# Landing tiles of an attention-and-FFN kernel laid out at a pitch of 256 bytes a row

## The chip, the cores and the metric

One core of a Trainium2 chip runs the whole program. The metric is the device time of one execution in microseconds (us). Fast runs of one kernel beside each other differ by 0.3% to 1.5% here, so each ratio below has its 95% interval. On one core there is no second die to compare with, so a run counts as slow when it is more than 1.5% above the fastest of the same kernel.

## The reference

The first half is a gated linear recurrence over 768 tokens, for 4 batches of 8 heads of width 48. The second half is a feed-forward net with a squared ReLU over the 3,072 resulting rows of 384 numbers.

```python
f = 1 / (1 + exp(-f_logit))                       # all of shape [4, 8, 768, 48], float32
for t in range(768):
    state = f[:, :, t, :, None] * state + k[:, :, t] (outer) v[:, :, t]
    y[:, :, t] = q[:, :, t] @ state
x = y.transpose(0, 2, 1, 3).reshape(3072, 384)
out = (relu(x @ w_in) ** 2) @ w_out               # w_in [384, 2048], w_out [2048, 384]
```

## The kernel before

The kernel works on 24 chunks of 128 tokens. For each chunk it loads four tiles (f, k, q, v), each by one DMA issued from SyncE. A partition holds one token, and the token's 8 heads are 8 rows of 48 floats. In HBM these 8 rows lie far apart (the layout is batch, head, token, width), so **every load is 1,024 separate rows of 192 bytes**, 64 for each of the 16 DMA engines. In SBUF the 8 rows of a token follow one another without gaps, 1,536 bytes in all. There are six buffers for each of the four tiles.

```python
C, H, D, DP = 128, 8, 48, 64
const = ctx.enter_context(tc.tile_pool(name="const", bufs=1))
io = ctx.enter_context(tc.tile_pool(name="io", bufs=IOB))          # IOB = 6
wst = ctx.enter_context(tc.tile_pool(name="wst", bufs=WSTB))
...
def load(i):
    b, c = divmod(i, NC)
    for n in ("f", "k", "q", "v"):
        def fn(n=n):
            t = io.tile([C, H, D], F32, tag="io_" + n, name="io_" + n)
            nc.sync.dma_start(t, srcs[n][b].rearrange("h s d -> s h d")[c * C:(c + 1) * C])
            st[n, i] = t
...
# the readers of the four tiles
nc.scalar.activation(e, st["f", i].rearrange("p h d -> p (h d)"), AFT.Exp, scale=-1.0)
nc.gpsimd.tensor_copy(vz[i % 3], st["v", i])
nc.vector.tensor_mul(az[i % 2][:, H:, :D], st["k", i], st["ep", i])
nc.vector.tensor_mul(az[i % 2][:, :H, :D], st["q", i], st["en", i][:, :HD].rearrange(...))
```

A planner in the kernel orders all steps ahead of time, so that attention chunks, the two matmuls of the net (`hp`, line 429, and `op`, line 474) and the weight loads interleave. The order on each engine is fixed when the program is built.

The tile pools are laid out one behind the other, and nothing rounds them to more than 32 bytes. The constants end at byte 52,896 of a partition, which is 206 × 256 + 160. All 24 landing tiles therefore begin at 160 modulo 256.

## Time and profile before

| | |
|---|---|
| time, median of 3 runs | 201.05 us (200.92 to 201.1) |
| span of the profiled run | 200.3 us |
| TensorE (PE) busy | 92% of the span |
| loads of f, k, q, v | 96 × 192 KB = 18.9 MB of the 29.9 MB in the queue |
| last of these loads issued | at 128.0 us |

These lines are from the page of the kernel before. The first two are 40 equal slices of the span, 5 us each: the busy share of the DMA engines in tenths, and the GB/s they moved. Then come the DMA queue (packets, MB, share of the 16 engines' span), two groups of instructions (busy us, mean ns of one | idle time before them and what ended most of it) and two of the DMA issues (the last number is the median us from issue to landing).

```profile
DMA  6999989899979999999989999931101111101012
GB/s 127 188 163 306 370 152 197 210 373 246 196 155 230 188 223 173 220 164 195 196 176 202 212 194 196 183 72 44 39 3 39 39 43 41 39 14 40 37 70 79
...
q1 hardware_dynamic: 107008, 29.89, 71.9%
...
L283 POOL CAST vz<-io_v 128x384 bf16<-128x384 f32 x24 | 14.7, 613 | 69.3 <-DMA io_v<-in_v_dram 50.6
L278 ACT ACTIVATE e<-io_f 128x384 f32<-128x384 f32 x24 | 12.6, 525 | 18.4 <-DMA io_f<-in_f_logit_dram 18.2
...
io_f<-in_f_logit_dram SPq DMA_DIRECT2D x24, 192.0 KB, 4.7
...
io_v<-in_v_dram SPq DMA_DIRECT2D x24, 192.0 KB, 4.5
```

For 130 us the DMA engines are nearly always busy, and then they have next to nothing to do. While they move rows of 192 B they reach about 150 to 230 GB/s. While they move the weights, in pieces of 1.5 to 2 KB, they reach about 370. ScalarE waits 18.2 us in all for f. GpSimd waits much longer for v, but it has little else to do.

The table by stretches of the same kernel gives the start and end of a stretch in us, its length, the busy us of PE (with the number of instructions) and of the other engines, the granted clock, the DMA share and GB/s. The DMA share adds up the times of the packets, which overlap, so it can be over 1.

```profile
core 0: us, PE busy (x) PEld busy (x) DVE busy (x) ACT busy (x) POOL busy (x), PEclk, DMA share, GB/s
...
48.00:78.00 30.00, 29.06 (x364) 20.84 (x363) 26.19 (x53) 21.16 (x46) 8.77 (x16) 1.00 1.00 191
78.00:106.00 28.00, 26.74 (x302) 18.16 (x300) 25.08 (x53) 22.55 (x51) 7.87 (x15) 1.00 1.03 191
106.00:130.00 24.00, 22.98 (x229) 15.05 (x228) 20.06 (x43) 17.22 (x40) 4.57 (x8) 1.00 1.18 197
```

Both TensorE and the DMA engines are close to full from 48 to 130 us. TensorE is the main limit, but it waits some 3.2 of these 82 us. This line of the timeline of SyncE's queue (start, duration) is the last load:

```profile
128.00 0.77 SPq L205 DMA_DIRECT2D io_v<-in_v_dram  x1
```

### The profile page before, as it was taken

The numbers are of one execution on the slowest core, as the hardware profiler recorded it, in microseconds if no ns is written. First come the engines' busy times: TensorE is split into PE (matmuls) and PEld (weight loads), VectorE is DVE, ScalarE is ACT, GpSimd is POOL, SyncE is SP. The second block draws the span as 40 slices with busy tenths as digits, with TensorE's granted clock in tenths as the row PEclk, the third lists the DMA queues.
The fourth block names the chain that finished last, engine by engine and source line by source line (L and its number), as shares of the span: only waits on it lengthen the run. The fifth ranks groups of instructions, "written<-read, shape, count | busy, mean of one in ns | idle before, by whom it ended". The sixth has DMA issues, their size and how long they took to land.

```text
span 200.3 us, 5054 instructions
## 1 busy us (share of the span) xinstructions
PE 183.7 (92%) x1965; PEld 128.5 (64%) x1965; DVE 141.1 (70%) x302; ACT 131.8 (66%) x279; POOL 39.5 (20%) x80
## 2 busy tenths in 40 slices
PE   5976898769989998999998999999999999999993
PEld 5855787657856665666665666666765666666651
DVE  3577878869869999898987779998855854333300
ACT  4462786669866578987977668678766565665410
POOL 5143001610133433114143031231400200000000
PEclk9999999999999999999999999999999999999999
DMA  6999989899979999999989999931101111101012
GB/s 127 188 163 306 370 152 197 210 373 246 196 155 230 188 223 173 220 164 195 196 176 202 212 194 196 183 72 44 39 3 39 39 43 41 39 14 40 37 70 79
DMA packets 107031, 30.20 MB, mean 151 GB/s; under 512 B 100352, under 2 KB 105472, under 8 KB 107008
## 3 DMA queue, kind: packets, MB, share of 16 engines
q1 hardware_dynamic: 107008, 29.89, 71.9%
q8 instruction: 15, 0.25, 0.5%
q14 instruction: 8, 0.07, 0.1%
HBM read 25.17 MB, written 4.72 MB: 149 GB/s over the span
## 4 chain that ended last, share of the span: by engine, by line
PE 45%; DMA 27%; SPq 19%; ACT 3%; issue 2%; POOL 1%; DVE 1%; POOLq 0%; ACTq 0%
PE op L474 20%; SPq L205 18%; PE hp L429 17%; DMA io_v<-in_v_dram 16%; DMA io_f<-in_f_logit_dram 11%; PE tr L321 2%; PE yp L359 2%; PE at L336 1%; SPq L221 1%; POOL vz L283 1%; PE pc L289 1%; ACT e L278 1%; PE xp L373 1%; ACT pz L279 1%; PE ds L390 1%
## 5 line engine op out<-in xcount | busy, mean ns | idle before, releaser
L429 PE MATMUL hp<-xT,w_in 128*128 128x384 bf16 (+2 forms) x528 | 78.9, 282 | 5.8 <-ACT hr L436 3.7
L474 PE MATMUL op<-w_out,hT 128*128 128x384 bf16 x384 | 77.5, 326 | 0.0
L436 ACT ACTIVATE hr<-hp 128x384 bf16<-128x384 f32 (+1 forms) x94 | 47.4, 509 | 22.7 <-PE hp L429 21.5
L429 PEld LDWEIGHTS <-w_in 128*128 128x128 bf16 x528 | 42.7, 98 | 23.2 <-issue 4.8
L445 DVE TENSOR_TENSOR hT<-hr 128x384 bf16<-128x384 bf16 (+1 forms) x91 | 34.9, 385 | 28.0 <-ACT hr L436 26.6
L474 PEld LDWEIGHTS <-hT 128*128 128x128 bf16 x384 | 35.4, 98 | 21.9 <-issue 1.0
L343 DVE TENSOR_TENSOR am<-at,ut 128x512 bf16<-128x512 f32 x48 | 31.7, 683 | 1.8 <-PE at L336 1.4
L407 POOL TENSOR_TENSOR sz<-tm,en 48x192 bf16<-48x192 f32 x40 | 21.5, 539 | 46.8 <-DVE tm L398 28.5
L283 POOL CAST vz<-io_v 128x384 bf16<-128x384 f32 x24 | 14.7, 613 | 69.3 <-DMA io_v<-in_v_dram 50.6
L278 ACT ACTIVATE e<-io_f 128x384 f32<-128x384 f32 x24 | 12.6, 525 | 18.4 <-DMA io_f<-in_f_logit_dram 18.2
L309 DVE TENSOR_TENSOR az<-io_k,ep 128x384 bf16<-128x384 f32 x24 | 13.7, 573 | 5.7 <-ACT ep L299 4.2
L321 PE MATMUL tr<-ident,az 128*128 128x128 bf16 x192 | 15.8, 223 | 1.4 <-DVE az L313 1.3
L438 DVE TENSOR_SCALAR hr<-hp 128x384 bf16<-128x384 f32 (+1 forms) x26 | 15.2, 588 | 2.2 <-PE hp L429 2.1
L443 ACT ACTIVATE hT<-hr 128x384 bf16<-128x384 bf16 (+1 forms) x29 | 15.9, 548 | 0.9 <-DVE hr L438 0.3
L321 PEld LDWEIGHTS <-az 128*128 128x128 bf16 x192 | 12.3, 100 | 4.4 <-DVE az L313 2.1
L327 DVE COPY ts<-tr 128x1024 bf16<-128x1024 bf16 x20 | 13.7, 684 | 1.7 <-PE tr L321 1.6
L313 DVE TENSOR_TENSOR az<-io_q,en 128x384 bf16<-128x384 f32 x24 | 14.1, 588 | 1.0 <-ACT en L305 0.7
L484 ACT COPY ob<-op 128x384 f32<-128x384 f32 x18 | 8.6, 477 | 9.4 <-PE op L474 9.3
L299 ACT ACTIVATE ep<-pc 128x384 f32<-128x384 f32 x24 | 11.7, 488 | 3.6 <-PE pc L292 3.6
L503 PE MATMUL idle<-zero 128*128 128x128 bf16 x141 | 13.1, 246 | 1.0 <-DVE zero L248 1.0
L279 ACT ACTIVATE pz<-e 128x384 bf16<-128x384 f32 x24 | 12.5, 523 | 0.8
L305 ACT ACTIVATE en<-pc 128x388 f32<-128x388 f32 (+1 forms) x24 | 11.9, 495 | 0.0
(43 smaller groups left out, 157.9 us busy)
## 6 DMA issues: line engine op xcount, KB each, us to landing
io_f<-in_f_logit_dram SPq DMA_DIRECT2D x24, 192.0 KB, 4.7
io_k<-in_k_dram SPq DMA_DIRECT2D x24, 192.0 KB, 4.5
io_q<-in_q_dram SPq DMA_DIRECT2D x24, 192.0 KB, 4.6
io_v<-in_v_dram SPq DMA_DIRECT2D x24, 192.0 KB, 4.5
out_dram<-ob SPq DMA_DIRECT2D x24, 192.0 KB, 1.9
wi_f<-in_moe_w_in_dram SPq DMA_DIRECT2D x4, 768.0 KB, 7.8
wo_f<-in_moe_w_out_dram SPq DMA_DIRECT2D x4, 768.0 KB, 8.1
```

What stands on the lines that cost most here:

```text
L205: nc.sync.dma_start(t, srcs[n][b].rearrange("h s d -> s h d")[c * C:(c + 1) * C])
L278: nc.scalar.activation(e, st["f", i].rearrange("p h d -> p (h d)"), AFT.Exp, scale=-1.0)
L283: nc.gpsimd.tensor_copy(vz[i % 3], st["v", i])
L321: nc.tensor.transpose(tr[:, y, :], a[:, 2 * y:2 * y + 2, :].rearrange("p h d -> p (h d)"), ident)
L343: nc.vector.tensor_mul(t, st["at", i][x], ut4)
L407: nc.gpsimd.tensor_mul(nx[r, :, D * x:D * (x + 1)], st["tm", i][r, :, D * x:D * (x + 1)], st["en", i][r, HD:HD + NP].unsqueeze(2).to_broad ...
L429: nc.tensor.matmul(hp[:, x, :], w_in[:, ks, (f + x) * C:(f + x + 1) * C], xT[:, ks, lo:lo + W], start=(ks == 0), stop=(ks == KS - 1), skip ...
L436: nc.scalar.activation(hr[:, :m, :], st["hp", c0, f][:, :m, :], AFT.Relu)
L438: nc.vector.tensor_scalar_max(hr[:, :m, :], st["hp", c0, f][:, :m, :], 0.0)
L443: nc.scalar.activation(st["hT", g][:, f:f + m, lo:lo + W], hr[:, :m, :], AFT.Square)
L445: nc.vector.tensor_mul(st["hT", g][:, f:f + m, lo:lo + W], hr[:, :m, :], hr[:, :m, :])
L474: nc.tensor.matmul(st["o", i], hT[:, fs, tt * C:(tt + 1) * C], w_out[:, fs, :], start=(fs == 0), stop=(fs == FS - 1))
```

## The change

The intent is that every row of 192 bytes begins at a multiple of 256 bytes in SBUF, so that no row is cut by a 256-byte line. The landing tile gets 64 floats a head instead of 48, and the last 16 stay unused. The activation of f can no longer read its tile as one flat run, so it takes 8 runs of 48.

```diff
-                t = io.tile([C, H, D], F32, tag="io_" + n, name="io_" + n)
+                t = io.tile([C, H, DP], F32, tag="io_" + n, name="io_" + n)[:, :, :D]
                 nc.sync.dma_start(t, srcs[n][b].rearrange("h s d -> s h d")[c * C:(c + 1) * C])
...
-            nc.scalar.activation(e, st["f", i].rearrange("p h d -> p (h d)"), AFT.Exp, scale=-1.0)
+            nc.scalar.activation(e.rearrange("p (h d) -> p h d", d=D), st["f", i], AFT.Exp, scale=-1.0)
```

## The prediction

> **What bounds the kernel now.** The change touches the 96 loads of q, k, v and f (18.9 of 29.9 MB) and their readers. In the timeline of the SyncE queue the last load is issued at 128.0 us. Until then the slices of the page show the DMA engines mostly at 90% or more, and the chain of waits gives 27% of the span to DMA and 18% to issuing loads. After 130 us only TensorE matters. But it is nearly full before too: in the table by stretches it is busy 29.1 of 30 us at 48-78 us, 26.7 of 28 at 78-106, 23.0 of 24 at 106-130. Counting matmul columns at the tail's rate (163 ns for 384), it does 92-93% of its possible work in those 82 us; gaps over 0.15 us sum to 4.4 us. So much faster loads would win some 4 us there, and an estimated 2 to 6 us in the first 48 us.
>
> **What the change does.** Number, size and order of the packets, their HBM addresses and the instruction order stay; only SBUF addresses move. The Trainium skill ("DMA: Bandwidth & Descriptors", How a descriptor splits into AXI transactions) says that transactions are cut at 256 B and that a read not starting at a multiple of 256 B fetches from the boundary below: the hope behind the change. Two things speak against it:
>
> 1. The tiles don't begin at a multiple of 256. In the address map of the program before, all 24 landing tiles begin at 160 modulo 256, and tiles of 2,048 B are not aligned either (az at 43,936). Rows now begin at 160, 96, 32 and 224: three of four cross a 256-byte line. With the padding I expect all at 160 and all to cross. The alignment would not be reached; any cost of crossing would grow.
>
> 2. Crossing shows no cost. Of 98,304 packets of 192 B in the trace's records 68,656 (70%) took the same 15 ns, which could not be if three of four paid a second transaction. At 50-60 us, with the queue not backed up, 0 to 4% are over 17 ns; where many loads are queued (8-12, 120-124 us) 70% are: slowness follows load, not address. At the start one engine begins a packet every 11.8 ns, through all four offsets.
>
> **Readers.** The activation of f becomes 8 runs of 48: ScalarE's other one of the pair already writes such runs, in 523 ns against 525 (the costliest groups). VectorE's products (573, 588 ns) and GpSimd's cast (613 mean, 512 median) read 8 runs instead of one: an estimate of 0 to 20 ns each, under 1 us of VectorE in all, off the chain. GpSimd is 20% busy.
>
> **Predicted time.** 201.2 us, 8 in 10 between 200.3 and 202.4. Faster by over 2%: 0.03; within 2%: 0.93; slower by over 2%: 0.04.
>
> **What would show it.** Packets of 192 B keep their peak at 15 ns and their mean of 18 (+-0.7) ns; issue to landing stays 4.4-4.8 us; last load issued at 127-130 us; TensorE's busy time in the three stretches within 0.5 us; the activation of f within 10 ns of 525, the cast within 30 ns of its mean.
>
> **What would make it wrong.** Writes that drain behind the records: if the slow 30% come from SBUF writes cut in two, crossing all rows would add some 5% to the loads (an estimate: a quarter more crossings at 3.5 ns, over 18 ns), 2 to 4 us. Had the allocator aligned the tiles after all, the same mechanism would win as much. An issue of the padded pattern that takes SyncE much longer than now (0.65 to 1.1 us) would also delay loads.

## The result, and the profile after

| | before | after |
|---|---|---|
| time, median of 4 runs | 200.99 us | 207.48 us (207.38 to 208.79) |
| ratio of the fast runs | 1 | 1.0344 (1.0299 to 1.039) |
| span of the profiled run | 200.3 us | 205.6 us |
| packets of 192 B: mean | 18.0 ns | 22.3 ns |
| packets of 192 B that took 15 ns | 70% | 44% |
| last load issued | 128.0 us | 134.6 us |

A ratio here is the mean time of one kernel's fast runs over that of the other's of the same rounds, so it is not quite the ratio of the medians beside it. The packet figures are counted from the trace's records of single DMA packets.

The kernel got 3.4% slower. All its engines run the same instructions in the same order as before, so only durations and waits can differ. These are the same lines of the page after.

```profile
DMA  7999999999989999999999999991011110101122
GB/s 120 163 142 273 380 166 176 157 386 269 196 164 201 195 199 168 191 175 198 164 191 175 203 175 175 193 169 44 0 41 38 38 38 5 40 36 41 38 77 77
...
q1 hardware_dynamic: 107008, 29.89, 83.4%
...
L283 POOL CAST vz<-io_v 128x384 bf16<-128x384 f32 x24 | 15.0, 626 | 78.9 <-DMA io_v<-in_v_dram 46.6
...
L278 ACT ACTIVATE e<-io_f 128x384 f32<-128x384 f32 x24 | 12.6, 525 | 24.1 <-DMA io_f<-in_f_logit_dram 24.0
...
io_f<-in_f_logit_dram SPq DMA_DIRECT2D x24, 192.0 KB, 5.1
...
io_v<-in_v_dram SPq DMA_DIRECT2D x24, 192.0 KB, 5.0
```

The number of packets and the bytes are the same, and the time that the packets took rose from 71.9 to 83.4% of a longer span. The readers did not change: the activation of f takes 525 ns as before, and the cast of v 626 against 613. ScalarE now waits 24.0 us for f instead of 18.2. A load takes 5.0 to 5.2 us to land instead of 4.5 to 4.7.

The table by stretches after:

```profile
core 0: us, PE busy (x) PEld busy (x) DVE busy (x) ACT busy (x) POOL busy (x), PEclk, DMA share, GB/s
...
48.00:78.00 30.00, 27.59 (x354) 19.90 (x352) 24.42 (x50) 19.82 (x43) 7.84 (x13) 1.00 1.16 193
78.00:106.00 28.00, 26.07 (x282) 17.39 (x281) 24.79 (x52) 21.72 (x50) 7.11 (x14) 1.00 1.38 180
106.00:130.00 24.00, 22.12 (x224) 14.40 (x222) 18.41 (x40) 17.60 (x41) 4.96 (x9) 1.00 1.23 182
```

And the last load, in the timeline of SyncE's queue:

```profile
134.59 1.16 SPq L205 DMA_DIRECT2D io_v<-in_v_dram  x1
```

TensorE lost 1.5, 0.7 and 0.9 us of work in these three stretches. Together with the three stretches before 48 us it was busy 116.7 us of the first 130 before and 111.3 after, which is 5.4 us less. From 130 to 150 us TensorE is busy without a gap in both kernels (20.00 of 20 us), and the missing work is simply done later: the span grew by 5.3 us. (The medians are 6.5 us apart. The profiled execution of the kernel before took 202.05 us, 1 us over its median.) So the time went into slower loads, and it reached the end through work that TensorE could not yet do.

### The profile page after: what moved, and what is told of

Its sections match the earlier page's. It is cut to its first block, busy times and chain, and to the rows that moved or that the text cites. A ratio compares the mean times of both kernels' runs of the same rounds, so it can differ in the third digit from the quotient of the medians.

```text
span 205.6 us, 5054 instructions
## 1 busy us (share of the span) xinstructions
PE 183.6 (89%) x1965; PEld 127.2 (62%) x1965; DVE 141.8 (69%) x302; ACT 131.5 (64%) x279; POOL 39.4 (19%) x80
## 3 DMA queue, kind: packets, MB, share of 16 engines
q1 hardware_dynamic: 107008, 29.89, 83.4%
## 4 chain that ended last, share of the span: by engine, by line
PE 46%; DMA 25%; SPq 21%; ACT 3%; issue 2%; POOL 1%; DVE 1%; POOLq 0%; ACTq 0%
PE op L474 21%; SPq L205 20%; PE hp L429 17%; DMA io_v<-in_v_dram 12%; DMA io_f<-in_f_logit_dram 8%; DMA wo_f<-in_moe_w_out_dram 5%; PE tr L321 2%; PE at L336 1%; PE yp L359 1%; SPq L221 1%; POOL vz L283 1%; PE xp L373 1%; PE pc L289 1%; ACT e L278 1%; PE ds L390 1%
## 5 line engine op out<-in xcount | busy, mean ns | idle before, releaser
L429 PEld LDWEIGHTS <-w_in 128*128 128x128 bf16 x528 | 42.7, 98 | 22.3 <-issue 3.5
L321 PEld LDWEIGHTS <-az 128*128 128x128 bf16 x192 | 11.9, 98 | 4.6 <-DVE az L313 1.9
L289 PE MATMUL pc<-pz,ut 128*128 128x384 bf16 x24 | 7.9, 328 | 7.7 <-ACT pz L279 4.5
L503 PE MATMUL idle<-zero 128*128 128x128 bf16 x141 | 12.2, 235 | 1.0 <-DVE zero L248 1.0
```

What stands on the lines that cost most here:

```text
L321: nc.tensor.transpose(tr[:, y, :], a[:, 2 * y:2 * y + 2, :].rearrange("p h d -> p (h d)"), ident)
L429: nc.tensor.matmul(hp[:, x, :], w_in[:, ks, (f + x) * C:(f + x + 1) * C], xT[:, ks, lo:lo + W], start=(ks == 0), stop=(ks == KS - 1), skip ...
```

## The experiments

A row of 192 bytes that begins at byte r of a 256-byte line crosses into the next one when r is over 64. With tiles at 160 modulo 256, the rows of the kernel before begin at 160, 96, 32 and 224 in turn, and **three of four cross**. At a pitch of 256 they all begin at 160, and **all cross**. The address map of the program after shows this: its 24 landing tiles still begin at 160 modulo 256. The change did not do what it set out to do.

Three theories of the slowdown were tested:

- **A.** A row that crosses a 256-byte line in SBUF costs the writing side of a DMA engine more.
- **B.** Boundaries of 64 bytes matter. All rows of both kernels begin off them.
- **C.** The gaps or the power-of-two pitch cost, wherever the rows begin.

The first four kernels ran beside the kernel before (median 201.03 us of 7 runs).

### Padded, tiles at 0 modulo 256

The edit to the changed kernel puts 96 unused bytes ahead of the landing tiles, and 160 behind so that everything else keeps its place modulo 256.

```diff
+    sh1 = ctx.enter_context(tc.tile_pool(name="sh1", bufs=1))
+    sh1.tile([C, 24], F32, name="sh1")
     io = ctx.enter_context(tc.tile_pool(name="io", bufs=IOB))
+    sh2 = ctx.enter_context(tc.tile_pool(name="sh2", bufs=1))
+    sh2.tile([C, 40], F32, name="sh2")
```

> The change with its landing tiles begun at 0 modulo 256 instead of 160 (96 unused bytes ahead, 160 behind so that nothing else moves): rows at 0, none crosses a 256-byte line. Theory A (a row that crosses a 256-byte line costs the DMA engine extra): mean packet of 192 B down to 15-16 ns, time 197 to 200 us, faster than before, since no row crosses instead of three of four. Theory B (a row not on a 64-byte boundary costs): the same as A here. Theory C (landing with gaps, at a pitch of 256 B, costs, wherever the rows begin): still 206 to 208 us and a mean packet of 22 ns.

Measured: 197.49 us, ratio to before 0.9783 (0.9705 to 0.9861), with one of its four runs (201.17 us) slow and left out of the ratio. The mean packet took 15.5 ns. From its page:

```profile
GB/s 130 215 171 356 337 182 196 291 378 146 211 164 194 231 213 172 232 205 212 198 197 235 198 218 213 123 12 34 40 40 16 27 42 43 40 40 40 30 54 80
...
q1 hardware_dynamic: 107008, 29.89, 65.0%
...
L282 ACT ACTIVATE e<-io_f 128x384 f32<-128x384 f32 x24 | 12.6, 526 | 8.8 <-DMA io_f<-in_f_logit_dram 8.8
...
io_v<-in_v_dram SPq DMA_DIRECT2D x24, 192.0 KB, 3.8
```

With 96 bytes of filler the same padded kernel goes from 3.4% slower to 2.2% faster than before. The wait for f falls to 8.8 us, and a load lands in 3.8 us. Theory C is refuted: pitch and gaps are the same as in the slow version. So is another fear of the prediction, that SyncE takes longer to issue the padded pattern: its issues of v took 0.81 us (median) before, 1.03 after the change, and 0.80 here with the same pattern.

### Padded, tiles at 128 modulo 256

The edit is the same with 224 bytes ahead and 32 behind. Every row crosses, and every row begins on a 64-byte boundary.

> The change with its landing tiles begun at 128 modulo 256: every row crosses a 256-byte line, and every row begins on a 64-byte boundary. Theory A (256-byte lines): as slow as the change, 206 to 208 us, mean packet 21 to 23 ns. Theory B (64-byte boundaries): as fast as with tiles at 0, 197 to 200 us. Theory C (pitch): 206 to 208 us.

Measured: 207.82 us, ratio 1.0321 (1.0266 to 1.0375), mean packet 21.8 ns.

```profile
q1 hardware_dynamic: 107008, 29.89, 81.6%
...
io_v<-in_v_dram SPq DMA_DIRECT2D x24, 192.0 KB, 5.1
```

It is as slow as the change. Theory B alone is refuted.

### A pitch of 320 bytes

The edit to the changed kernel is one number. The tiles begin at 160 as in the change, and the rows begin at 160, 224, 32 and 96: the four offsets of the kernel before, but with gaps.

```diff
-                t = io.tile([C, H, DP], F32, tag="io_" + n, name="io_" + n)[:, :, :D]
+                t = io.tile([C, H, 80], F32, tag="io_" + n, name="io_" + n)[:, :, :D]
```

> The change with rows at a pitch of 320 B instead of 256, tiles at 160 modulo 256: rows begin at 160, 224, 32 and 96, the four offsets of the kernel before, but with gaps between the rows as in the change. Theory A: three of four cross, as before: 200 to 202 us, mean packet 18 ns. Theory B: as before too. Theory C (gaps): 206 to 208 us.

Measured: 200.89 us, ratio 1.0002 (0.993 to 1.0074), mean packet 18.6 ns. Gaps, larger tiles and readers with 8 runs show no cost together. The share of crossing rows is enough to give the old time.

### Unpadded, tiles at 0 modulo 256

The edit is that of the first experiment (96 bytes ahead, 160 behind), made to the kernel before. Two of four rows cross.

> The kernel before, unpadded, with its landing tiles begun at 0 modulo 256: rows at 0, 192, 128 and 64, so two of four cross a 256-byte line instead of three, and all begin on 64-byte boundaries. Theory A: mean packet near 16.5 ns, between that with tiles at 0 padded and that of before, 198 to 200.5 us. Theory B: as fast as the padded kernel with tiles at 0. Theory C: as before, 201 us.

Measured: 196.8 us, ratio 0.9787 (0.9726 to 0.9847), mean packet 15.5 ns.

```profile
q1 hardware_dynamic: 107008, 29.89, 65.7%
...
L282 ACT ACTIVATE e<-io_f 128x384 f32<-128x384 f32 x24 | 12.6, 526 | 9.7 <-DMA io_f<-in_f_logit_dram 9.7
...
io_v<-in_v_dram SPq DMA_DIRECT2D x24, 192.0 KB, 3.7
```

This was not foreseen by A in its simple form: with half the rows crossing, the loads were as fast as with none. B would explain it, but B alone had just failed. Either both boundaries matter, or the cost of crossing is hidden as long as few enough rows cross. The loads alone and the padded tiles at 32 tell these apart.

### Loads alone

This is a kernel without arithmetic, whose output is zeros and so wrong. Sixteen stages of 24 loads follow one another, of the same form as in the kernel, and the stages differ only in where the rows begin.

```python
for name, src, off, pitch in STAGES:
    for j in range(24):
        a = ...     # the load's 128 x 8 rows of 192 B in HBM
        t = slots[j][:, off // 4:off // 4 + 8 * pitch // 4].rearrange("p (h w) -> p h w", w=pitch // 4)[:, :, :48]
        nc.sync.dma_start(t, a)
```

> No arithmetic and a wrong result on purpose: 16 stages of 24 loads each, back to back, each load 128 partitions of 8 rows of 192 B as in the kernel; the stages differ only in where a row begins in SBUF (0, 32, ... 224 modulo 256 at a pitch of 256; a pitch of 192 from 0 and from 160) and in HBM (back to back as now; at a pitch of 256 from 0, 64, 128). Theory A (a row that crosses a 256-byte line in SBUF costs the writing side of an engine more; hidden while the mean stays below what the reading side needs): a load takes some 0.9 to 1.0 us with rows at 0, 32 and 64, 10 to 25% more with rows at 96 to 224 (all cross), 0 to 3% more at pitch 192 from 0 (two of four cross), 3 to 8% more at pitch 192 from 160 (three of four). Theory B (64-byte boundaries as well): rows at 32 slower than at 0 and 64 by 5% or more, and rows at 128 and 192 faster than at 96, 160 and 224. If the reading side is the floor and pays for crossings in HBM, rows that cross none there are faster than now by 5% or more with rows at 0 in SBUF, and rows that all cross there are slower.

From its table by stretches, one row inside each stage (DVE and POOL do nothing; the last two numbers are the DMA share and GB/s). The first nine rows are: pitch 256 from 0, 32, 64, 96, 128, 160 and 224 modulo 256, then pitch 192 from 0 and pitch 192 from 160. The next two have rows at 0 in SBUF while in HBM they are at a pitch of 256 from 0 (no row crosses there) and from 128 (all cross there). The last row repeats the first stage.

```profile
core 0: us, DVE busy (x) POOL busy (x), PEclk, DMA share, GB/s
6.00:22.00 16.00, 0.00 (x0) 0.00 (x0) 1.00 1.09 215
28.00:44.00 16.00, 0.00 (x0) 0.00 (x0) 1.00 1.07 210
50.00:66.00 16.00, 0.00 (x0) 0.00 (x0) 1.00 1.09 214
77.00:95.00 18.00, 0.00 (x0) 0.00 (x0) 1.00 1.54 163
105.00:124.00 19.00, 0.00 (x0) 0.00 (x0) 1.00 1.53 163
134.00:152.00 18.00, 0.00 (x0) 0.00 (x0) 1.00 1.51 163
...
192.00:210.00 18.00, 0.00 (x0) 0.00 (x0) 1.00 1.50 163
217.00:233.00 16.00, 0.00 (x0) 0.00 (x0) 1.00 1.10 211
240.00:258.00 18.00, 0.00 (x0) 0.00 (x0) 1.00 1.39 187
...
264.00:280.00 16.00, 0.00 (x0) 0.00 (x0) 1.00 1.05 213
...
338.00:352.00 14.00, 0.00 (x0) 0.00 (x0) 1.00 1.14 217
...
388.00:404.00 16.00, 0.00 (x0) 0.00 (x0) 1.00 1.09 214
```

A load is 196,608 bytes, so 215 GB/s is 0.915 us a load, 163 is 1.205 us and 187 is 1.05 us. The step lies between rows at 64 and rows at 96, where 192 bytes begin to cross a line. On either side of it the starting byte makes no difference that shows: 32 is within 2.5% of 0 and 64, and 128 is as bad as 96, 160 and 224. That settles A against B. (Rows that cross nothing all take the 0.915 us of a floor that the last run of loads explains, so a smaller effect of the first byte could be hidden there.) The sizes given to A were too small: all rows crossing cost 32% where 10 to 25% were expected, three of four 15% where 3 to 8% were. What the rows do in HBM shows no effect at this rate.

The numbers also suggest why half the rows may cross for nothing. All rows crossing take 1.205 us / 64 = 18.8 ns a row and engine. If a row that crosses nothing takes half, 9.4 ns, then three of four give 16.5 ns, or 1.054 us a load, and 1.05 was measured. Two of four give 14.1 ns, or 0.904 us, which is just under the 0.915 us that a load takes anyway.

### Padded, tiles at 32 modulo 256

The edit is the same with 128 bytes ahead and 128 behind. No row crosses, and none begins on a 64-byte boundary.

> The change with its landing tiles begun at 32 modulo 256: no row crosses a 256-byte line, none begins on a 64-byte boundary. Theory A: as with tiles at 0, 196 to 198.5 us, mean packet 15.5 ns. Theory B, or a mix in which 64-byte boundaries matter too (which would explain why unpadded tiles at 0 did as well as padded ones): 199 us or more, mean packet over 16.5 ns.

Measured beside the kernel before (201.29 us): 197.09 us, ratio 0.9774 (0.9723 to 0.9824), mean packet 15.5 ns. In the whole kernel too, 64-byte boundaries don't matter.

### Unpadded, tiles at 0, and the weights' tiles too

The edit to the kernel before is its shortest good form: the two lines of `sh1` alone.

> The unpadded kernel with landing tiles at 0 modulo 256, the filler of 160 bytes behind them left out, so that the weights' staging tiles begin at 0 modulo 256 too. It repeats the best version in its simplest form. Theory A: 196 to 198 us; the eight weight loads gain at most a nanosecond or two of 84 a packet, so no more than 0.5 us better than with the filler.

Measured: 197.71 us, ratio 0.9795 (0.9743 to 0.9847). Moving the weights' staging tiles to 0 modulo 256 adds nothing that can be seen.

### Shares of crossing rows

Loads alone again (wrong output), with 0, 3, 4, 5, 6, 7 and 8 of 8 rows crossing, by pitches of 256, 272, 192, 288, 192, 272 and 256 from suitable bytes. After these come stages with loads issued by SyncE and ScalarE in turn.

> Loads alone again, a wrong result on purpose: 12 stages of 24 loads, with 0, 3, 4, 5, 6, 7 and 8 of a load's 8 rows a partition crossing a 256-byte line (by pitch and first byte), and four of these shares again with the loads issued by SyncE and ScalarE in turn. From the first measurement alone (0.915 us a load with no row crossing, 1.205 with all) the model is: the writing side takes 9.4 ns for a row that crosses no line and twice that, 18.8, for one that does, and a load takes the larger of 64 rows of that mean and a floor of 0.915 us. It expects, in us a load: 0.92 with 0, 3 and 4 of 8 crossing, 0.98 with 5, 1.05 with 6, 1.13 with 7, 1.205 with 8. Rival: the cost is not additive but a matter of some threshold or pattern; then 5, 6 and 7 of 8 lie off that line by over 0.02. For the floor: if it is SyncE's issuing, two queues bring none crossing down to 0.75-0.85 us and 4 of 8 only to 0.90; if it is the engines' reading, two queues leave both at 0.91-0.93. 8 of 8 stays at 1.205 in either case.

From its table by stretches, the rows for 4, 5, 6 and 7 of 8:

```profile
51.00:67.00 16.00, 0.00 (x0) 0.00 (x0) 1.00 1.07 212
73.00:90.00 17.00, 0.00 (x0) 0.00 (x0) 1.00 1.10 201
97.00:114.00 17.00, 0.00 (x0) 0.00 (x0) 1.00 1.43 187
122.00:142.00 20.00, 0.00 (x0) 0.00 (x0) 1.00 1.48 174
```

| crossing, of 8 | model, us a load | measured, 196,608 B over the GB/s |
|---|---|---|
| 0 | 0.92 | 0.93 |
| 3 | 0.92 | 0.93 |
| 4 | 0.92 | 0.93 |
| 5 | 0.98 | 0.978 |
| 6 | 1.05 | 1.051 |
| 7 | 1.13 | 1.130 |

The sum holds: 9.4 ns for a row, 18.8 for a crossing one, and a floor below which crossings are hidden. The other stages of this run failed as a measurement. ScalarE had nothing to wait for and issued its share of the later stages early, so that they mixed with the stage of 8 of 8. Their numbers are not used.

### What the floor is

This is the same kind of kernel with every load issued by SyncE and ScalarE in turn from the first on, in four pairs of stages.

```diff
-            nc.sync.dma_start(t, a)
+            (nc.scalar if j % 2 else nc.sync).dma_start(t, a)
```

> Loads alone, every load issued by SyncE and ScalarE in turn from the first on (in the run before, ScalarE's loads ran ahead into the stage of another share and mixed them). Pairs of stages of 24 loads: no row crossing, 4 of 8, 8 of 8, none again. If the floor of 0.915 us a load is one queue's issuing: none crossing 0.60 to 0.85 us a load, and 4 of 8 at 0.90 (64 rows of 14.1 ns), so that crossings show at half the rows too. If the floor is the engines' own reading: 0.91 to 0.93 for both. 8 of 8 stays at 1.205.

From its table by stretches: none crossing, 4 of 8, 8 of 8, and none again.

```profile
4.00:19.00 15.00, 0.00 (x0) 0.00 (x0) 1.00 1.28 259
...
62.00:79.00 17.00, 0.00 (x0) 0.00 (x0) 1.00 1.40 218
85.00:108.00 23.00, 0.00 (x0) 0.00 (x0) 1.00 1.51 163
...
160.00:174.00 14.00, 0.00 (x0) 0.00 (x0) 1.00 1.28 259
```

With two queues, none crossing takes 0.76 us a load, 4 of 8 takes 0.90 and 8 of 8 takes 1.205 as ever. So the floor of 0.915 us belongs to the use of one queue. Whether it is SyncE's own time to issue or something else in the queue is not shown: a second engine and a second queue came in together. Once the floor is gone, crossings cost at half the rows too, by the amount that the sum gives (0.904). What limits the loads at 0.76 us (11.9 ns a row) stays open: it is above the 0.60 us that 9.4 ns a row would allow.

### Padded and unpadded at 0, five rounds

The last two runs are the kernels of the first and the fourth experiment again, on one chip, with the kernel before at 200.25 us.

> The padded kernel with tiles at 0 modulo 256 again, beside the unpadded one with tiles at 0, on one chip: by the model their loads take the same (none and two of four rows crossing both lie at or under the floor of 0.915 us), so 196 to 198.5 us and within 0.5% of each other.

> The unpadded kernel with tiles at 0 modulo 256 again: 196 to 198.5 us, within 0.5% of the padded one. If it is clearly slower, half the rows crossing costs something in the kernel after all; if clearly faster, the padding costs something else (readers of 8 runs).

Measured: padded 196.77 us, ratio 0.9833 (0.9779 to 0.9888); unpadded 196.06 us, ratio 0.9796 (0.9747 to 0.9846). The intervals overlap, so no difference is shown, and the padding has nothing to its credit. Two lines that move the tiles by 96 bytes give all of the gain, at no cost in SBUF worth naming. The unpadded kernel with tiles at 0 is the one to keep. It beats both the kernel before and the change. (Each of these kernels is clearly faster than the one before, but every interval includes 0.98, so a gain of over 2% is not shown.) With two issuing queues the padding might earn its place, since none crossing then took 0.76 us a load against 0.90 with half; that was not tried in the whole kernel.

## Why the prediction was wrong

**Point 1 was right.** The prediction said from the address map that the tiles begin at 160 modulo 256, that the change would not align them and that all rows would cross instead of three of four. They do.

**Point 2, "Crossing shows no cost", is the step that failed.** It read the packet records: 70% of the packets took 15 ns, which "could not be if three of four paid a second transaction". That inference is unsound. In the changed kernel every row crosses, and still 44% of the packets took 15 ns. So the record of a single packet does not show what its own row costs. That the cost appears on other packets, as delay once the writing side is behind, fits this but is inferred: no record here separates reading from writing. "Slowness follows load, not address" could not be concluded either. Every stretch of the kernel before has the same mix, three of four rows crossing, so comparing its stretches says nothing about addresses. The packet every 11.8 ns "at the start" may show only how fast packets begin before the queue is full: with two queues each engine took 11.9 ns a row that crosses nothing. The reading that shows the cost is the rate where the queue is full, set beside that of other addresses. The second slice (5 us) of the page shows 188 GB/s before, 163 after and 215 with padded tiles at 0; the loads alone ran at 187, 163 and 215 with three of four, all and none crossing. The prediction had only the first of these rates; a kernel with other addresses was needed to read it.

**The fallback had the mechanism and too small a size.** "What would make it wrong" named writes cut in two and estimated 3.5 ns a crossing, 5% on the loads and 2 to 4 us. The runs gave 9.4 ns more for a crossing row and 1.05 to 1.205 us a load, which is 15%; the kernel lost 6.5 us. A quarter more crossings at 9.4 ns is 2.4 ns over 16.4, or 14%.

**How much of it reached the end.** The fallback's 5% are some 5 us of DMA time (96 × 1.05 × 0.05), of which it let 2 to 4 us, 40% to 80%, reach the end. The runs are at or just under the low end of that. Loads that are 15% longer are 96 × 0.155 = 15 us more of DMA time, of which 6.5 us (43%) reached the end. Fixed alignment saves 96 × 0.13 = 12 us of DMA time, of which 4.2 us (35%) reached the end (2.1% of 201.03 us by the ratio). The prediction's gain for much faster loads, some 4 us in the stretch of 48 to 130 us plus 2 to 6 us before it, was not tested: these loads were only 12% faster.

**Readers: right.** The activation of f stayed at 525 ns, and the cast of v moved by 13 ns. The other tests that the prediction set (mean packet, landing, last load, TensorE's busy time in the stretches) all failed in the direction of slower loads; only the commonest packet stayed at 15 ns.

The Trainium skill ("DMA: Bandwidth & Descriptors", How a descriptor splits into AXI transactions) says that transactions are cut at 256 B. The prediction cited it and then argued it away. The runs agree with a cut at 256 bytes on the SBUF side: twice the time (18.8 against the fitted 9.4 ns) as soon as a row of 192 bytes crosses, whatever the sizes of the two pieces (163 GB/s from 96, 128, 160 and 224 alike). That the doubling is one transaction against two is what the page suggests; no run here shows transactions as such.

## What to carry to other kernels

For loads in short rows, look at the byte address modulo 256 at which each row lands, in the program's address map, and count the rows that cross: a pitch aligns nothing unless the first byte is aligned, and here, with rows of 192 bytes, the only length measured, 96 bytes of filler decided between 3.4% slower and 2% faster than before. Judge DMA cost by bytes per us where the queue is full, never by the usual duration of a packet. And ask which limit hides the cost: with one issuing queue half the rows could cross for nothing, with two they could not.

## What the Trainium skill lacked or had wrong

- "DMA: Bandwidth & Descriptors" (How a descriptor splits into AXI transactions) describes what an unaligned start costs a read, and gives no cost for writes into SBUF. Here a row of 192 bytes that crosses a 256-byte line in SBUF took an engine 18.8 ns, and the rows that cross nothing fit 9.4 ns (inferred from 5, 6 and 7 of 8 crossing). A start at 32 or 64 was as good as at 0 (210 to 215 GB/s, all at the floor of one queue), and starts at 96 to 224 were equally slow (163).
- The same section has bytes before an unaligned start fetched on a read and costing beats. With one queue this was invisible: 213 GB/s with all rows of the source at 0 modulo 256 and 217 with all at 128. It may hide under the floor of one queue; this was not tried with two.
- "DMA: Bandwidth & Descriptors" (Issuing engines are not separate DMA queues) calls the issuing time that several engines save usually small relative to the DMA itself. For loads of 192 KB in rows of 192 B a second issuing engine, with its queue, raised the rate from 215 GB/s to 259, as long as no row crossed.
- "SBUF — State Buffer" (Operand start alignment) speaks of legality and says that its runs timed nothing. No page that was read warns that a tile of 2,048 bytes a partition need not start at a multiple of 256; all 24 began at 160.
